# Clustered attention with a mixture of experts: scores and maxima of two key blocks in three full PSUM banks instead of four of 384 columns

## The chip, the cores and the metric

The kernel runs on one core of one Trainium2 chip. The metric is the device time of one launch in microseconds, the median of several runs. Engines are named as in the profile: PE (TensorE matmul), PEld (its weight loads), DVE (VectorE), ACT (ScalarE), POOL (GpSimd), SP (the engine that issues most DMAs). A PSUM bank holds 512 float32 columns on 128 partitions; the kernel uses six banks as a ring and two for other sums.

## The reference

Attention over 4 batches of 8 heads (sequence 768, head size 64), where a query sees only keys of its own cluster, and behind it a mixture of 8 experts of which each token uses two:

```
q_assign = argmax(q_n @ c_n.T);  k_assign = argmax(k_n @ c_n.T)      # 16 clusters per head
mask   = q_assign[..., :, None] == k_assign[..., None, :]
scores = where(mask, scale * q @ k.T, -1e9)
attn   = exp(scores - max(scores)) / (sum + 1e-9)
x      = (attn @ v) as rows of 512
top2 of x @ w_gate + noise * log1p(exp(x @ w_noise)), softmax over the two
out[token] += weight * (relu(x @ w1[e]) @ w2[e])                     # for both experts of a token
```

## The kernel before, in words

**Stages.** The 32 heads are worked on as 16 pairs (`p`), two heads (`s`) each. Attention is one long list of steps (`attention`, L378 to L393): step `t` is one block of 128 keys (`kc`, six to a head) against all 768 queries, so a pair takes 12 steps and the stage 192. The experts follow (`experts`, L949 on); nothing in them is touched.

**One step.** `scores` (L633) computes for its key block the masked scores, less the row's maximum, of all queries: two PSUM tiles of 384 columns, each from two accumulating matmuls (L641, operands `A` and `Bt`), and for each an Exp on ACT into the float32 tile `pe` (L642; 768 columns in all, six such tiles in rotation). One to three steps later `split_p` (L645) has POOL, for the last 21 blocks DVE, compute `pl`, the part of `pe` that its bfloat16 upper half leaves (L653). Four steps after the scores `values` (L656) multiplies both halves with the values: 18 matmuls of 64 or 65 columns per block into the tile `av` (L670, L672, L676); two blocks of a head fall into one step.

**Maxima.** For a later pair `b_max` (L603) computes the masked scores the other way round (128 queries against 768 keys) in two tiles of 384 columns with one matmul each (L611), and DVE takes each tile's negated row maximum (L613). `b_neg` and `b_negT` (L615, L624) bring these maxima into two rows of `Bt` by a transpose and a DMA, which the pair's first scores wait for.

**The ring.** All these tiles, and those of transposes and of small reductions, are taken in turn from six banks (`ps`, L141). A matmul into a bank waits until the tile that was six places earlier has been read, by ACT (scores) or by DVE (maxima).

**What sets the order.** Each engine executes its instructions in the order in which the program is written. The table `AT` (L27) gives to every piece of side work a step, rounded to thirds; `at` files it under step and third. The loop at L378 writes, for each step: the first third's side work, `scores`, the splits of earlier blocks, the second third, `values`, the last third. `AT["bmax"]` and `["bstep"]` place `b_max` from 9.333 steps on, one query block per step.

Of the kernel before, what the change touches and what calls it, by code (L numbers as in the profile page):

```python
# [9 lines left out]
F32 = mybir.dt.float32  # L10
# [19 lines left out]
    L=4, qk=-20.667, v=-8.667,  # L30
    vscale=-0.667, vsplit=10.667, vstep=1.0, split=[-4.667, -3.667, -4.0, -3.333], place=-0.667,
    sims=[2.0, 2.667], scales=[-14.333, -13.333, -13.0, -10.0, -8.667], scales1=2.0, max1=3.333, ge=3.667, max2=4.333, eq=4.667, mask=6.333, bmask=6.333,
    bmax=9.333, neg=20.333, negT=22.0, zero=31.0, zstep=12.0, zlist=21.0, v1=4.0, store=2.667, turn=6.667, glog=12.0,
    xh=1.333, xh0=4.0, pause=4.0, list=[34.0, 34.0, 19.0], lstep=[2.0, 2.0, 1.1667], bstep=1.0,
    gate=[13.667, 13.667, 6.333], am=5.333, amstep=0.333, xs=6.0, ky=4.0, cut=[13, 20], gplace=[30.0, 30.0, 14.333],
    vd=[1, 1, 2, 3, 4, 5], sec=-6.0, qf=[0, -4.0], place1=4.333,
# [9 lines left out]
class Kernel:  # L46
# [170 lines left out]

    def centroids(self):
        nc, D, C = self.nc, self.D, self.C
        self.early = self.wk.tile([128, 2, 384], F32, name="pe", bufs=6).rearrange("p a n -> p (a n)")  # L220
        o = 128 + 4 * C
        c1 = self.early[:, o:o + D]
        c2 = self.c2 = self.early[:, o + D:o + 3 * D].rearrange("p (a d) -> p a d", d=D)
        nc.sync.dma_start(c1, self.cent.rearrange("h c d -> (h c) d"))
        self.constants()
        n = self.early[:, o + 3 * D:o + 3 * D + 3]
        nc.vector.tensor_mul(c2[:, 0, :], c1, c1)
        nc.vector.reduce_sum(n[:, 0:1], c2[:, 0, :], axis=X)
        self.rnorm(n[:, 0:1], n[:, 1:3])
        nc.vector.tensor_scalar(c2, c1[:, None, :].to_broadcast([128, 2, D]), n[:, 0:1], None, op0=OP.mult)  # L230
# [14 lines left out]
    def attention(self, ctx):  # L245
# [20 lines left out]
        def at(step, f, *a):  # L266
            sched.setdefault(divmod(round(3 * step), 3), []).append((f, a))
# [7 lines left out]
        for p in range(NP):  # L275
            b, hp = divmod(p, H // 2)
            w = 12 * (p - 2)
            if hp == 0:
                for g in range(2):
                    at(w + T["qk"] + 24 * g + (0 if b else T["qf"][g]), self.load_qk, b, g)  # L280
                    v = w + 24 * g
                    V = T["fv"][g] if p == 0 else T
                    at(v + V["v"] + (T["v1"] if (b, g) == (1, 0) else 0), self.load_v, b, g)
                    at(v + V["vscale"], self.v_sizes, b, g)
                    chain(v + V["am"], V["amstep"], self.v_scale(b, g))
                    if g:
                        fs = self.x_scale(b)
                        chain(v + V["xs"] - (4 if b else 0), 1.0 if b else 0.333, fs[:-1])
                        at(v + V["xs"] + (2.667 if b else 3.333), fs[-1])
                    for h in range(0, 4, 2):  # L290
                        at(v + V["vsplit"] + V["vstep"] * (h + 0.667), self.v_split, b, g, h)
            P = T["first"] if p == 0 else T
            w += (0, T["sec"], T["thr"])[p] if p < 3 else 0
            if p == 0:
                for i in range(4):
                    at(w - 7.0, self.a_turn, p, i // 2, i % 2)
            if p < 2 or p % 2 == 0:
                fs = self.scales(p, 2 if p < 2 else 4)
                for x, f in zip(P["scales"], fs):
                    at(w + x + (T["scales1"] if p == 1 else 0), f)  # L300
            for i in range(4):
                at(w + P["split"][i], self.a_halves if p == 0 else self.a_split, p, i // 2, i % 2)
            if p == 0:
                at(w + P["sims"][0], self.c_turn)
            at(w + P["place"] + (T["place1"] if p == 1 else 0), self.b_place, p)
            for s in range(2):
                at(w + P["sims"][s], self.a_sims, p, s)
            for k, f in (("max1", self.a_max1), ("ge", self.a_ge), ("ky", self.a_ky), ("max2", self.a_max2),
                         ("eq", self.a_eq), ("mask", self.a_mask), ("bmask", self.b_mask)):
                at(w + P[k], f, p)  # L310
            if p == 0:
                for s in range(2):
                    for j in range(NJ):
                        at(w + P["bmax"][s] + P["bstep"][s] * j, self.b_max, p, s, j)
                    at(w + P["neg"][s], self.b_neg, p, s, 1)
                    at(w + P["negT"][s], self.b_negT, p, s, 1)
            else:
                w = 12 * (p - 2)
                bm, bs = (T["bmax1"], T["bstep1"]) if p == 1 else (T["bmax"], T["bstep"])
                for s in range(2):  # L320
                    for j in range(NJ):
                        at(w + bm + bs * (6 * s + j), self.b_max, p, s, j)
                at(w + T["neg"], self.b_neg, p, 0, 2)
                at(w + T["negT"] + (T["thr"] if p == NP - 1 else 0), self.b_negT, p, 0, 2)
            w = 12 * (p - 2)
            z = w + 36 + L
            if p + 1 < NP:
                at(z + T["xh"] + (T["xh0"] if p == 0 else 0), self.x_halves, p)
                at(z + T["store"] + (T["xh0"] if p == 0 else 0), self.store_x, p)
                turn, glog = (T["store"], 6.333) if p == NP - H // 2 - 1 else (T["turn"], T["glog"]) if p < NP - 2 else (5.0, 8.0)  # L330
                at(z + turn, self.turn_h, p)
                if p < NP - 2:
                    at(z + glog, self.g_logits, p)
            if hp == H // 2 - 1:
                if b + 1 == B:
                    continue
                fs = self.g_gate(b)
                chain(z + T["gate"][b], 0.333, fs[:8])
                for i, f in enumerate(fs[8:self.GP]):
                    x = T["gate"][b] + 2.667 + (0.333 if b < 2 else 0.1667) * i  # L340
                    at(z + x + (T["pause"] if b < 2 and x > 21 else 0), f)
                chain(z + T["gplace"][b], 0.1667, fs[self.GP:])
                for j in range(2 * NJ):
                    at(z + T["list"][b] + T["lstep"][b] * j, self.g_list, b, j)
# [7 lines left out]
        z = 12 * NP  # L352
# [25 lines left out]
        for t in range(min(sched)[0], z + L + 2):  # L378
            u = t - L
            slot = lambda i: [f(*a) for f, a in sched.pop((t, i), [])]  # L380
            slot(0)
            if 0 <= t < z:
                self.scores(t // 12, (t % 12) // 6, t % 6)
            for x in range(t - 3, t):
                if 0 <= x < z and t - x == (1 if x < z - 19 or x > z - 12 else 3 if x < z - 15 else 2):
                    self.split_p(x // 12, (x % 12) // 6, x % 6)
            slot(1)
            if 0 <= u < z:
                p, s, kc = u // 12, (u % 12) // 6, u % 6
                for i in range(NJ):  # L390
                    if AT["vd"][i] == kc:
                        self.values(p, s, i)
            slot(2)  # L393
        assert not sched

    def fixed_init(self, i):
# [203 lines left out]
                self.dma(A[64:80, i, :, 384 * a:384 * a + 384], mk[64 * i + 32 * a:64 * i + 32 * a + 16],  # L600
                         self.nc.scalar if a and p < 5 else None)

    def b_max(self, p, s, j):  # L603

        nc, st, A = self.nc, self.st[p], self.A[p % 3]
        if (s, j) == (0, 0):
            st["mm"] = self.wk.tile([128, 2 * self.NJ, 2], F32, name="mm")
        c = self.NJ * s + j
        for n in range(2):
            t = self.ps()[:, :384]  # L610
            nc.tensor.matmul(t, A[:, 0, s, j * 128:j * 128 + 128],  # L611
                             A[:, 1, s, n * 384:n * 384 + 384], start=True, stop=True)
            nc.vector.tensor_reduce(st["mm"][:, c, n:n + 1], t, axis=X, op=OP.max, negate=True)  # L613

    def b_neg(self, p, s, n):  # L615

        v, W, c = self.nc.vector, n * self.NJ, self.NJ * s
        o = self.aux[:, 500 + c:500 + c + W]
        hi, lo = (self.nm[:, W * i:W * i + W] for i in range(2))
        v.tensor_reduce(o, self.st[p]["mm"][:, c:c + W], axis=X, op=OP.min)  # L620
        v.tensor_scalar(hi, o, 1.0 / MASK, None, op0=OP.mult)
        v.scalar_tensor_tensor(lo, hi, -MASK, o, op0=OP.mult, op1=OP.add)

# [6 lines left out]
        self.dma(self.Bt[p % 3][96:98, 1, s:s + n], nt[:W], None if p else nc.scalar)  # L630


    def scores(self, p, s, kc):  # L633
        nc, st, A, Bt = self.nc, self.st[p], self.A[p % 3], self.Bt[p % 3]
        ks = slice(kc * 128, kc * 128 + 128)
        pe = self.wk.tile([128, 2, 384], F32, name="pe", bufs=6)
        for n in range(2):
            t = self.ps()[:, :384]
            ns = slice(n * 384, n * 384 + 384)
            for M, qi in ((A, 0), (Bt, 1)):  # L640
                nc.tensor.matmul(t, M[:, 1 - qi, s, ks], M[:, qi, s, ns], start=not qi, stop=bool(qi))  # L641
            nc.scalar.activation(pe[:, n], t, AF.Exp, bias=math.log(64.0), scale=st["sc"][:, 4:5])  # L642
        st["p", s, kc] = pe

    def split_p(self, p, s, kc):  # L645

        nc, st = self.nc, self.st[p]
        pe = st["p", s, kc].rearrange("p a n -> p (a n)")
        hi = pe.bitcast(BF).rearrange("p (n two) -> p n two", two=2)[:, :, 1]
        lo = self.wk.tile([128, self.S], F16, name="pl", bufs=5)  # L650

# [679 lines left out]
```

## Time and profile before

| | before |
|---|---|
| median of 3 runs (range) | 1014.69 us (1014.54 to 1014.77) |
| the profiled execution's own time | 1013.59 us |
| its span in the trace | 1011.8 us |
| granted TensorE clock, mean | 0.976 of full |
| PE, DVE, ACT, POOL busy | 92%, 65%, 47%, 56% of the span |
| attention steps | about 43 to 461 us of the span |
| experts | about 461 us to the end |

The span is what the trace covers; the execution's own time is 1.8 us more. A busy PE is not PE at its peak, since matmuls overlap in the records. The chain that ended last is followed backwards from the last instruction; its shares tell which work's duration stood on the path, not how busy an engine was.

### The profile page before, as it was taken

Reading aid. Unit: us, or ns where it says so; the run is one execution under the profiler, and the core shown is the slowest. Engines: PE = TensorE matmul, PEld = TensorE weight load, DVE = VectorE, ACT = ScalarE, POOL = GpSimd, SP = SyncE. Lnnn points to the kernel's source line nnn. Section 1 sums busy time; section 2 is a strip of 40 time slices with the busy share of each in tenths; the row PEclk is TensorE's granted clock in tenths of the full one; section 3 lists DMA queues with packets and bytes.
Section 4 is the critical chain, followed back from the end, with each engine's and each line's share of the span. In section 5 each row is a group of like instructions: output and inputs, shape, how many; then the busy total and the mean of one; then the engine's idle time right before and its main releaser. Section 6 shows DMA issues by size and latency. Waiting matters only on the chain.

```text
span 1011.8 us, 22606 instructions
## 1 busy us (share of the span) xinstructions
PE 928.7 (92%) x8825; PEld 560.4 (55%) x8825; DVE 660.6 (65%) x1485; ACT 473.4 (47%) x896; POOL 565.7 (56%) x608
## 2 busy tenths in 40 slices
PE   4588989898899987889999999999999999999997
PEld 3356666666666664668555445455454454554543
DVE  6688777888678876897556465365564654655631
ACT  4578788888787865674032224123131241231310
POOL 9268797979997899853456125242261252422312
PEclk7699999999999998999999999999999999999999
DMA  6543767666667444668377645655665356555201
GB/s 178 125 118 89 194 156 185 183 165 145 179 153 189 119 95 98 204 152 176 109 150 242 137 142 167 140 174 149 173 193 140 126 165 152 172 151 155 73 24 46
DMA packets 181905, 148.84 MB, mean 147 GB/s; under 512 B 93543, under 2 KB 159079, under 8 KB 181794
## 3 DMA queue, kind: packets, MB, share of 16 engines
q1 hardware_dynamic: 167990, 110.73, 43.8%
q0 software_dynamic: 13296, 36.38, 11.7%
q8 instruction: 70, 1.15, 0.5%
q10 hardware_dynamic: 508, 0.25, 0.1%
q14 instruction: 41, 0.34, 0.1%
HBM read 81.80 MB, written 26.12 MB: 107 GB/s over the span
## 4 chain that ended last, share of the span: by engine, by line
PE 57%; POOL 10%; DVE 9%; issue 9%; ACT 6%; DMA 4%; SPq 0%; ACTq 0%; POOLq 0%; DVEq 0%
PE ring L1230 21%; PE ring L1270 20%; POOL pl L653 6%; PE ring L641 5%; ACT pe L642 3%; DVE mm L613 3%; PE ring L611 2%; POOL tbl L899 2%; DMA B<-nt 2%; PE av L670 1%; PE av L676 1%; PE av L672 1%; POOL out L1283 1%; PE ring L1260 1%; DVE pl L653 1%
## 5 line engine op out<-in xcount | busy, mean ns | idle before, releaser
L653 POOL TENSOR_TENSOR pl<-pe 128x768 f16<-128x768 f32 x171 | 247.9, 1468 | 47.4 <-ACT pe L642 41.9
L1230 PE MATMUL ring<-xT,w1t 128*128 128x404 f16 (+2 forms) x1632 | 267.1, 324 | 0.0
L1270 PE MATMUL ring<-w2t,hT 128*128 128x512 f16 x1152 | 250.8, 379 | 0.5 <-DVE w2t L1166 0.5
L642 ACT ACTIVATE pe<-ring,sc 128x384 f32<-128x384 f32 x384 | 200.0, 577 | 69.1 <-PE ring L641 62.0
L613 DVE TENSOR_REDUCE mm<-ring 128x1 f32<-128x384 f32 x384 | 192.1, 549 | 44.6 <-PE ring L611 44.0
L1283 POOL DMA_INDIRECT out<-yo,idx x52 | 58.7, 1129 | 285.4 <-DVE yo L1279 209.3
L1230 PEld LDWEIGHTS <-w1t 128*128 128x128 f16 x1632 | 157.4, 97 | 106.4 <-issue 2.5
L1270 PEld LDWEIGHTS <-hT 128*128 128x128 f16 x1152 | 112.4, 98 | 135.0 <-issue 1.2
L1239 ACT ACTIVATE hT<-ring 128x404 f16<-128x404 f32 (+2 forms) x136 | 57.6, 469 | 202.1 <-PE ring L1230 201.9
L641 PE MATMUL ring<-B 128*128 128x384 f16 x384 | 127.2, 332 | 3.6 <-DMA B<-nt 3.6
L641 PE MATMUL ring<-A 128*128 128x384 f16 x384 | 126.8, 330 | 3.6 <-ACT pe L642 2.1
L611 PE MATMUL ring<-A 128*128 128x384 f16 x384 | 105.2, 334 | 16.5 <-ACT pe L642 8.0
L1240 DVE SCALAR_TENSOR_TENSOR hT<-ring,hT 128x404 f16<-128x404 f32 (+2 forms) x136 | 66.7, 529 | 73.5 <-ACT hT L1239 73.5
L1279 DVE SCALAR_TENSOR_TENSOR yo<-ring,lsw,xt 128x512 f32<-128x512 f32 (+1 forms) x49 | 36.7, 748 | 110.2 <-PE ring L1270 104.3
L670 PE MATMUL av<-vv,pe 128*128 128x65 f16 x1152 | 96.9, 194 | 7.5 <-DVE xt L685 7.4
L672 PE MATMUL av<-vv,pe 128*128 128x64 f16 x1152 | 96.9, 193 | 0.0
L670 PEld LDWEIGHTS <-pe 128*128 128x128 bf16 x1152 | 83.7, 98 | 22.9 <-issue 9.3
L1165 ACT ACTIVATE w1t<-stg,ws 128x1024 f16<-128x1024 f32 x32 | 34.5, 1139 | 121.2 <-DVE ws L170 121.2
L672 PEld LDWEIGHTS <-pe 128*128 128x128 bf16 x1152 | 78.4, 99 | 11.3 <-issue 4.7
L676 PE MATMUL av<-vv,pl 128*128 128x65 f16 x1152 | 66.8, 194 | 5.6 <-POOL pl L653 4.2
L1210 POOL DMA_INDIRECT xh<-xs,idx x52 | 56.4, 1085 | 16.5 <-issue 15.0
L1154 DVE TENSOR_REDUCE wm<-stg 128x1 f32<-128x1024 f32 x56 | 65.5, 1208 | 0.0
(227 smaller groups left out, 1171.0 us busy)
## 6 DMA issues: line engine op xcount, KB each, us to landing
stg<-in_moe_w SPq DMA_DIRECT2D x64, 512.0 KB
vt<-in_v SPq DMA_DIRECT2D x8, 768.0 KB
out<-zt SPq DMA_DIRECT2D x12, 512.0 KB
A<-hl SPq DMA_DIRECT2D x30, 192.0 KB
B<-hl SPq DMA_DIRECT2D x30, 192.0 KB
xs<-xh SPq DMA_DIRECT2D x15, 384.0 KB
qk<-in_q SPq DMA_DIRECT2D x7, 768.0 KB
qk<-in_k SPq DMA_DIRECT2D x7, 768.0 KB
```

The source lines that it names most:

```text
L611: nc.tensor.matmul(t, A[:, 0, s, j * 128:j * 128 + 128], A[:, 1, s, n * 384:n * 384 + 384], start=True, stop=True)
L613: nc.vector.tensor_reduce(st["mm"][:, c, n:n + 1], t, axis=X, op=OP.max, negate=True)
L641: nc.tensor.matmul(t, M[:, 1 - qi, s, ks], M[:, qi, s, ns], start=not qi, stop=bool(qi))
L642: nc.scalar.activation(pe[:, n], t, AF.Exp, bias=math.log(64.0), scale=st["sc"][:, 4:5])
L653: (nc.vector if last else nc.gpsimd).tensor_tensor(lo, pe, hi, op=OP.subtract)
L670: nc.tensor.matmul(av[:, j, :], ph[:, js], vv[:, hh, kj, 64:129], start=(kc == 0 and j == 0), stop=False, skip_group_check=True)
L672: nc.tensor.matmul(av[:, j, :64], ph[:, js], vv[:, hh, kj, 0:64], start=False, stop=False, skip_group_check=True)
L676: nc.tensor.matmul(av[:, j, :], pl[:, js], vv[:, hh, kj, 64:129], start=False, stop=(kc == NJ - 1), skip_group_check=True)
L1230: nc.tensor.matmul(p, self.w1t[:, wi, c, f * 128:f * 128 + 128], self.xT[:, c, xi, n0:n1], start=(i == 0), stop=(i == 3 * ND - 1))
L1240: nc.vector.scalar_tensor_tensor(h1, x, 0.0, h0, op0=OP.max, op1=OP.subtract)
L1270: nc.tensor.matmul(p, self.hT[:, hi, f, t * 128:t * 128 + 128], self.w2t[:, wi, f], start=(i == 0), stop=(i == 3 * NF - 1))
L1283: i = nc.gpsimd.indirect_dma_start(out=self.out, out_offset=bass.IndirectOffsetOnAxis(ap=en[:r], axis=0), in_=yo[:r], in_offset=None, boun ...
```

## The change

Two key blocks of a head now share one `pe` tile of 1536 columns (four in rotation instead of six of 768) and three PSUM tiles of 512 columns: the first holds 512 queries' columns of the even block, the second the even block's last 256 and the odd block's first 256, the third the odd block's last 512. `pieces` yields the parts of a tile. Each tile gets one Exp of 512 columns. The three tiles are written at three places: the first at the start of the even step, the second at its end, the third in the odd step behind the splits. `b_max` does the same for two query blocks: three tiles of 512 columns, one reduction each (the middle tile's gives two columns of maxima), placed every 2/3 of a step instead of two tiles every step; `AT["bmax"]` becomes 9.0. `b_neg` reads the same 24 maxima, laid out flat. `early` is the tile of `pe`'s name that the constants use at the start.

```diff
-    bmax=9.333, neg=20.333, negT=22.0, zero=31.0, ...
+    bmax=9.0, neg=20.333, negT=22.0, zero=31.0, ...
...
-                    for j in range(NJ):
-                        at(w + bm + bs * (6 * s + j), self.b_max, p, s, j)
+                    for j in range(3 * NJ // 2):
+                        at(w + bm + bs * (9 * s + j) * 2 / 3, self.b_max, p, s, j)
...
-            if 0 <= t < z:
-                self.scores(t // 12, (t % 12) // 6, t % 6)
+            score = lambda i: 0 <= t < z and self.scores(t // 12, (t % 12) // 6, t % 6 // 2, i)
+            if t % 2 == 0:
+                score(0)
             for x in range(t - 3, t):
                 if 0 <= x < z and t - x == (1 if x < z - 19 or x > z - 12 else 3 if x < z - 15 else 2):
                     self.split_p(x // 12, (x % 12) // 6, x % 6)
+            if t % 2:
+                score(2)
             slot(1)
...
             slot(2)
+            if t % 2 == 0:
+                score(1)
...
+    def pieces(self, c, i):
+        S = self.S
+        x = 512 * i
+        while x < 512 * i + 512:
+            y = min(512 * i + 512, (x // S + 1) * S)
+            yield c + x // S, x % S, x - 512 * i, y - x
+            x = y
...
-        for n in range(2):
-            t = self.ps()[:, :384]
-            nc.tensor.matmul(t, A[:, 0, s, j * 128:j * 128 + 128],
-                             A[:, 1, s, n * 384:n * 384 + 384], start=True, stop=True)
-            nc.vector.tensor_reduce(st["mm"][:, c, n:n + 1], t, axis=X, op=OP.max, negate=True)
+        jj, i = divmod(q, 3)
+        t = self.ps()
+        for j, x, o, n in self.pieces(2 * jj, i):
+            nc.tensor.matmul(t[:, o:o + n], A[:, 0, s, j * 128:j * 128 + 128], A[:, 1, s, x:x + n], start=True, stop=True,
+                             skip_group_check=True)
+        c = 2 * self.NJ * s + 4 * jj + (0, 1, 3)[i]
+        k = 2 if i == 1 else 1
+        nc.vector.tensor_reduce(st["mm"][:, c:c + k], t.rearrange("p (k n) -> p k n", k=k), axis=X, op=OP.max, negate=True)
...
-        pe = self.wk.tile([128, 2, 384], F32, name="pe", bufs=6)
-        for n in range(2):
-            t = self.ps()[:, :384]
-            ns = slice(n * 384, n * 384 + 384)
-            for M, qi in ((A, 0), (Bt, 1)):
-                nc.tensor.matmul(t, M[:, 1 - qi, s, ks], M[:, qi, s, ns], start=not qi, stop=bool(qi))
-            nc.scalar.activation(pe[:, n], t, AF.Exp, bias=math.log(64.0), scale=st["sc"][:, 4:5])
-        st["p", s, kc] = pe
+        if i == 0:
+            pe = self.wk.tile([128, 2 * S], F32, name="pe", bufs=4)
+            for k in range(2):
+                st["p", s, 2 * kk + k] = pe[:, S * k:S * k + S]
+            st["pe"] = pe
+        t = self.ps()
+        for kc, x, o, n in self.pieces(2 * kk, i):
+            ks = slice(kc * 128, kc * 128 + 128)
+            for M, qi in ((A, 0), (Bt, 1)):
+                nc.tensor.matmul(t[:, o:o + n], M[:, 1 - qi, s, ks], M[:, qi, s, x:x + n], start=not qi, stop=bool(qi),
+                                 skip_group_check=True)
+        nc.scalar.activation(st["pe"][:, 512 * i:512 * i + 512], t, AF.Exp, bias=math.log(64.0), scale=st["sc"][:, 4:5])
```

How it moves PE's instructions. Before, in an attention step of a late pair (the scores of one key block, L641, then the maxima of one query block, L611; `A` and `Bt`, here B, are the operands, each matmul behind its weight load):

```order
L641 LDWEIGHTS A_132
L641 MATMUL ring<-A_132 128x384
L641 LDWEIGHTS B_135
L641 MATMUL ring<-B_135 128x384
L641 LDWEIGHTS A_132
L641 MATMUL ring<-A_132 128x384
L641 LDWEIGHTS B_135
L641 MATMUL ring<-B_135 128x384
L611 LDWEIGHTS A_133
L611 MATMUL ring<-A_133 128x384
L611 LDWEIGHTS A_133
L611 MATMUL ring<-A_133 128x384
```

With the change, at the turn from an even to an odd step: the middle tile of the scores (L660, two parts of 256), a tile of maxima (L625) and the third tile of the scores, whose second matmul, of B, follows:

```order
L660 LDWEIGHTS A_132
L660 MATMUL ring<-A_132 128x256
L660 LDWEIGHTS B_135
L660 MATMUL ring<-B_135 128x256
L660 LDWEIGHTS A_132
L660 MATMUL ring<-A_132 128x256
L660 LDWEIGHTS B_135
L660 MATMUL ring<-B_135 128x256
L625 LDWEIGHTS A_133
L625 MATMUL ring<-A_133 128x512
L660 LDWEIGHTS A_132
L660 MATMUL ring<-A_132 128x512
```

Two tiles of scores now stand close together around a tile of maxima, with no matmuls of `values` between them; the even block is complete only with the middle tile. The number of matmuls is the same.

On ACT, over some steps in which it also builds the next pair's mask (L577), its operand halves (L524) and a row of maxima (L629). Before:

```order
L642 ACTIVATE pe<-ring,sc 128x384 x2
L577 ACTIVATE mk<-ring,ms 128x768
L642 ACTIVATE pe<-ring,sc 128x384 x2
L524 ACTIVATE hl<-ring,sc 128x384 x2
L642 ACTIVATE pe<-ring,sc 128x384 x2
L524 ACTIVATE hl<-ring,sc 128x384 x2
L642 ACTIVATE pe<-ring,sc 128x384 x2
L629 ACTIVATE nt<-ring 24x128
```

With the change (the same places are L662, L582, L529 and L645):

```order
L662 ACTIVATE pe<-ring,sc 128x512
L582 ACTIVATE mk<-ring,ms 128x768
L662 ACTIVATE pe<-ring,sc 128x512 x2
L529 ACTIVATE hl<-ring,sc 128x384 x2
L662 ACTIVATE pe<-ring,sc 128x512
L529 ACTIVATE hl<-ring,sc 128x384 x2
L662 ACTIVATE pe<-ring,sc 128x512 x2
L645 ACTIVATE nt<-ring 24x128
```

Where ACT had two Exps in every step, it has one in even and two in odd steps.

## Rows read from the trace of the kernel before

**Rows 1.** Windows: engine busy us (instructions), granted clock, DMA share, GB/s, by stretch.

```profile
core 0: us, PE busy (x) PEld busy (x) DVE busy (x) ACT busy (x) POOL busy (x), PEclk, DMA share, GB/s
43.00:461.00 418.00, 368.74 (x5686) 263.87 (x5686) 343.14 (x891) 318.36 (x593) 344.40 (x297) 0.98 0.62 152
...
235.00:280.00 45.00, 37.66 (x560) 27.16 (x557) 34.54 (x91) 34.94 (x65) 43.01 (x46) 1.00 0.67 163
...
337.00:385.00 48.00, 42.24 (x673) 30.98 (x670) 36.03 (x92) 33.30 (x62) 46.04 (x48) 0.98 0.53 118
...
461.00:1011.00 550.00, 541.17 (x2997) 283.36 (x2994) 291.26 (x525) 135.23 (x266) 193.66 (x282) 1.00 0.52 143
```

**Rows 2.** Chain that ended last: whole span, then 100 to 235, then 235 to 280.

```profile
by line: PE ring L1230 21.4%; PE ring L1270 20.0%; issue 8.5%; POOL pl L653 5.7%; PE ring L641 4.5%; ACT pe L642 3.2%; DVE mm L613 2.5%; PE ring L611 2.3%; POOL tbl L899 1.6%; DMA B<-nt 1.5%; PE av L670 1.5%; PE av L676 1.4%; PE av L672 1.4
...
by line: PE ring L641 16.7%; ACT pe L642 9.8%; PE ring L611 8.4%; DMA B<-nt 8.2%; issue 5.3%; PE av L670 4.7%; PE av L676 4.6%; PE av L672 4.5%; DVE mm L613 3.4%; PE ring L511 3.4%; DMA qk<-in_q 3.2%; ACT junk L178 3.1%; ACT hl L524 2.5%; D
...
by line: POOL pl L653 58.1%; POOL tbl L899 18.4%; POOL xh L721 7.1%; issue 6.0%; ACT pe L642 3.6%; PE ring L641 1.9%; DVE xt L685 1.3%; PE av L670 0.7%; POOL ch L455 0.6%; DVE rs L682 0.5%; POOL spacer L898 0.5%; DVE rs L683 0.5%; PE ring L
```

**Rows 3.** Costliest groups: shapes, count | busy us, mean ns | idle before, releasers.

```profile
L653 POOL TENSOR_TENSOR pl<-pe 128x768 f16<-128x768 f32 x171 | 247.9, 1468 | 47.4 <-ACT pe L642 41.9 <-ACT nt L629 2.2 <-ACT gm L829 2.1
L642 ACT ACTIVATE pe<-ring,sc 128x384 f32<-128x384 f32 x384 | 200.0, 577 | 69.1 <-PE ring L641 62.0 <-POOL pl L653 3.8 <-PE ring L611 1.7
L613 DVE TENSOR_REDUCE mm<-ring 128x1 f32<-128x384 f32 x384 | 192.1, 549 | 44.6 <-PE ring L611 44.0
```

**Rows 4.** Waits, 43 to 461: engine line <- releaser: us, times, longest us.

```profile
ACT pe L642 <- PE ring L641: 62.0, 77, 2.2
...
PEld L641 <- issue: 21.5, 64, 1.4
PEld L611 <- issue: 9.8, 24, 1.4
...
PE ring L611 <- ACT pe L642: 8.0, 24, 1.1
...
PEld L676 <- POOL pl L653: 5.1, 7, 1.0
...
PE av L676 <- POOL pl L653: 4.2, 6, 0.9
...
PE ring L641 <- ACT pe L642: 2.1, 3, 1.2
...
PE ring L611 <- DVE mm L613: 1.5, 2, 1.1
```

**Rows 5.** Groups by form: other lengths from PSUM on ACT and DVE.

```profile
L1239 ACT ACTIVATE hT<-ring 128x404 f16<-128x404 f32 x56 | 28.5, 508 | 169.5 <-PE ring L1230 169.5
...
L1239 ACT ACTIVATE hT<-ring 128x256 f16<-128x256 f32 x24 | 8.8, 381 | 32.5 <-PE ring L1230 32.4
...
L160 DVE TENSOR_REDUCE pr<-ring 128x1 f32<-128x128 f32 x15 | 4.2, 281 | 0.0
```

**Rows 6.** Timeline: start us, us, engine line op, count [idle before]; a full ring.

```profile
127.40 1.98 ACT L642 ACTIVATE pe<-ring,sc 128x384 f32<-128x384 f32 x4
...
128.02 0.32 PE L611 MATMUL ring<-A 128*128 128x384 f16 x1 [1.06 <-ACT pe L642]
...
138.84 3.07 DVE L613 TENSOR_REDUCE mm<-ring 128x1 f32<-128x384 f32 x6
```

**Rows 7.** Pieces of the chain: start us, us, what; matmuls of 384, 256 and 512 columns.

```profile
164.25 0.65 PE ring L641 x4
...
460.63 7.87 PE ring L1230 x72
...
492.27 15.55 PE ring L1270 x72
```

More of the change, by code (lines that the diff above doesn't have):

```diff
@@ L32 @@
     sims=[2.0, 2.667], scales=[-14.333, -13.333, -13.0, -10.0, -8.667], scales1=2.0, max1=3.333, ge=3.667, max2=4.333, eq=4.667, mask=6.333, bmask=6.333,
-    bmax=9.333, neg=20.333, negT=22.0, zero=31.0, zstep=12.0, zlist=21.0, v1=4.0, store=2.667, turn=6.667, glog=12.0,
+    bmax=9.0, neg=20.333, negT=22.0, zero=31.0, zstep=12.0, zlist=21.0, v1=4.0, store=2.667, turn=6.667, glog=12.0,
     xh=1.333, xh0=4.0, pause=4.0, list=[34.0, 34.0, 19.0], lstep=[2.0, 2.0, 1.1667], bstep=1.0,
@@ L219, in centroids @@
         nc, D, C = self.nc, self.D, self.C
-        self.early = self.wk.tile([128, 2, 384], F32, name="pe", bufs=6).rearrange("p a n -> p (a n)")
+        self.early = self.wk.tile([128, 2 * self.S], F32, name="pe", bufs=4)
         o = 128 + 4 * C
@@ L312, in attention @@
                 for s in range(2):
-                    for j in range(NJ):
-                        at(w + P["bmax"][s] + P["bstep"][s] * j, self.b_max, p, s, j)
+                    for j in range(3 * NJ // 2):
+                        at(w + P["bmax"][s] + P["bstep"][s] * j * 2 / 3, self.b_max, p, s, j)
                     at(w + P["neg"][s], self.b_neg, p, s, 1)
@@ L320, in attention @@
                 for s in range(2):
-                    for j in range(NJ):
-                        at(w + bm + bs * (6 * s + j), self.b_max, p, s, j)
+                    for j in range(3 * NJ // 2):
+                        at(w + bm + bs * (9 * s + j) * 2 / 3, self.b_max, p, s, j)
                 at(w + T["neg"], self.b_neg, p, 0, 2)
@@ L601, in b_mask, with b_max @@
                          self.nc.scalar if a and p < 5 else None)
-    def b_max(self, p, s, j):
-        nc, st, A = self.nc, self.st[p], self.A[p % 3]
-        if (s, j) == (0, 0):
-            st["mm"] = self.wk.tile([128, 2 * self.NJ, 2], F32, name="mm")
-        c = self.NJ * s + j
-        for n in range(2):
-            t = self.ps()[:, :384]
-            nc.tensor.matmul(t, A[:, 0, s, j * 128:j * 128 + 128],
-                             A[:, 1, s, n * 384:n * 384 + 384], start=True, stop=True)
-            nc.vector.tensor_reduce(st["mm"][:, c, n:n + 1], t, axis=X, op=OP.max, negate=True)
+    def pieces(self, c, i):
[5 more added lines that the diff above has]
+            x = y
+    def b_max(self, p, s, q):
+        nc, st, A = self.nc, self.st[p], self.A[p % 3]
+        if (s, q) == (0, 0):
+            st["mm"] = self.wk.tile([128, 4 * self.NJ], F32, name="mm")
+        jj, i = divmod(q, 3)
[6 more added lines that the diff above has]
+        nc.vector.tensor_reduce(st["mm"][:, c:c + k], t.rearrange("p (k n) -> p k n", k=k), axis=X, op=OP.max, negate=True)
     def b_neg(self, p, s, n):
@@ L619, in b_neg @@
         hi, lo = (self.nm[:, W * i:W * i + W] for i in range(2))
-        v.tensor_reduce(o, self.st[p]["mm"][:, c:c + W], axis=X, op=OP.min)
+        v.tensor_reduce(o, self.st[p]["mm"][:, 2 * c:2 * c + 2 * W].rearrange("p (j n) -> p j n", n=2), axis=X, op=OP.min)
         v.tensor_scalar(hi, o, 1.0 / MASK, None, op0=OP.mult)
@@ L630, in b_negT, with scores @@
         self.dma(self.Bt[p % 3][96:98, 1, s:s + n], nt[:W], None if p else nc.scalar)
-    def scores(self, p, s, kc):
-        nc, st, A, Bt = self.nc, self.st[p], self.A[p % 3], self.Bt[p % 3]
-        ks = slice(kc * 128, kc * 128 + 128)
-        pe = self.wk.tile([128, 2, 384], F32, name="pe", bufs=6)
-        for n in range(2):
-            t = self.ps()[:, :384]
-            ns = slice(n * 384, n * 384 + 384)
+    def scores(self, p, s, kk, i):
+        nc, st, A, Bt, S = self.nc, self.st[p], self.A[p % 3], self.Bt[p % 3], self.S
+        if i == 0:
[6 more added lines that the diff above has]
+            ks = slice(kc * 128, kc * 128 + 128)
             for M, qi in ((A, 0), (Bt, 1)):
-                nc.tensor.matmul(t, M[:, 1 - qi, s, ks], M[:, qi, s, ns], start=not qi, stop=bool(qi))
-            nc.scalar.activation(pe[:, n], t, AF.Exp, bias=math.log(64.0), scale=st["sc"][:, 4:5])
-        st["p", s, kc] = pe
+                nc.tensor.matmul(t[:, o:o + n], M[:, 1 - qi, s, ks], M[:, qi, s, x:x + n], start=not qi, stop=bool(qi),
+                                 skip_group_check=True)
+        nc.scalar.activation(st["pe"][:, 512 * i:512 * i + 512], t, AF.Exp, bias=math.log(64.0), scale=st["sc"][:, 4:5])
     def split_p(self, p, s, kc):
         nc, st = self.nc, self.st[p]
-        pe = st["p", s, kc].rearrange("p a n -> p (a n)")
+        pe = st["p", s, kc]
         hi = pe.bitcast(BF).rearrange("p (n two) -> p n two", two=2)[:, :, 1]
```

## The prediction

> **What bounds the kernel now.** I read the windows first. From 461 us on PE is busy in 541 of 550 us [rows 1]: the experts are PE's, the change touches nothing there, and what attention gains or loses passes on whole. In the attention steps, 43 to 461 us, nobody is full: of 418 us PE is busy 369, POOL 344, DVE 343, ACT 318 [rows 1]. So no engine's total sets this stage; four engines in fixed orders hand tiles to each other, and which hand-over ends last changes from stretch to stretch.
>
> Next the chain of waits. Over the span it lies 4.5% on the matmuls of the scores, 3.2% on the Exp, 2.5% on the reductions of the maxima, 2.3% on their matmuls [rows 2]. Between 100 and 235 us it runs to and fro between PE and ACT; between 235 and 280 it is POOL's, 58.1% on the splits alone [rows 2], with POOL busy for 43.0 of 45 us, and 337 to 385 looks the same with 46.0 of 48 [rows 1]. These 93 us the change can hardly touch: POOL's splits stay as they are, 171 of 1468 ns [rows 3].
>
> Last the waits. ACT's Exp waited for PE 77 times, 62.0 us in all, yet PE also waited for ACT to empty a bank: 24 times, 8.0 us, before a matmul of the maxima, 2.1 us before one of the scores, and 1.5 us for DVE [rows 4], 11.6 us together. One such place is plain: at 127.40 ACT comes out of other work with four Exps in a row, and PE, its six banks full, stands still for 1.06 us until one is free [rows 6]. Each side waits for the other at times; that is what a short ring between two engines with uneven side work looks like.
>
> **The change part by part.**
>
> *Exp.* 384 of 384 columns become 288 of 512. No Exp of 512 stands in this trace. Between 256 and 404 columns an ACT read of PSUM goes from 381 to 508 ns, 0.86 ns a column [rows 5]; 128 more columns make 577 [rows 3] into 687 ns. Two key blocks cost 4 x 577 = 2308 ns before and 3 x 687 = 2061 after, 10.7% less. Back to back the four take 1.98 us [rows 6], (1.98 - 0.577) / 3 = 468 ns for each further one; 4 x 468 against 3 x 578 is 7.4% less. The chain has 3.2% of 1011.8 = 32.4 us of Exp, so the path shortens by 2.4 to 3.5 us; I take **3.5**, since most Exps there follow a wait. Outer ends: nothing (ACT off the path), or 96 pairs of blocks x 0.247 = 23.7 us if ACT alone bound the stage, which its 318 of 418 us excludes.
>
> *Reductions.* From 128 to 384 columns a reduction goes from 281 [rows 5] to 549 ns [rows 3], 1.05 ns a column, so 512 take 683: 3 x 683 against 4 x 549 is 6.7% less. In a row of six each further one takes (3.07 - 0.55) / 5 = 504 ns [rows 6]; 3 x 638 against 4 x 504 is 5% less. Of 2.5% = 25.3 us on the chain that is 1.3 to 1.7 us; I take **1.5**. The shorter end of a pair's last maxima, one reduction where two stood, is in it.
>
> *The ring.* In two steps scores and maxima took eight tiles and now take six: the whole ring turns once in two steps, and PE may run a third more columns ahead of the slower reader. PE's visible waits for a bank are 11.6 us. Between nothing and all of it I take a quarter, **3**, because the same moments are partly counted as Exp on the chain. The weight loads held back by "issue", 21.5 and 9.8 us [rows 4], have no releaser in the records; I give them no price.
>
> *A longer hand-over.* Against this, ACT must now wait for a full bank: two matmuls of 512 columns instead of 384. Four of 384 take 0.65 us, 72 of 512 take 15.55 [rows 7]: 2 x 216 = 432 ns against 325, 107 more. If every wait of ACT for PE (77, of which three quarters are left) stood on the path, this would cost 58 x 0.107 = 6.2 us. But ACT's waits are mostly PE's own busy time (`values`, side matmuls), when nobody loses; I take **1**.
>
> *PE's work.* Same number of matmuls and weight loads, same columns. Parts of 256 run at 7.87 / 72 = 109 ns, 0.43 ns a column, as 384 and 512 do (0.42) [rows 7]: nothing, and no cover is needed.
>
> *Tiles and order.* A `pe` tile comes back after eight steps instead of six, which can only help the 3.8 us that the Exp waited for POOL's split [rows 3]; nothing counted. The even block is complete with the middle tile, at the end of its step instead of its start, so its split can start about a step later. It is used four steps after the scores, and POOL takes 1468 ns a block where a step lasts 418 / 192 = 2.18 us. Where POOL is behind it does not wait, and where it is not, some two steps are left. Nothing counted; what hides it is that reserve. If it ran out, `values` would wait for `pl`, which now costs 5.1 + 4.2 = 9.3 us [rows 4].
>
> Sum: -3.5 - 1.5 - 3 + 1 = **-7.0 us** of the profiled execution's 1013.59, so 1006.6. That execution is 1.1 us under the median of the runs; against the median the forecast is 1014.69 - 7.0 = **1007.7 us**.
>
> **A rule that speaks against it.** ACT is busy 76% and DVE 82% of the stage [rows 1], and both still hold PE up at times [rows 4]. The Trainium skill (Perfetto Trace Analysis, Optimizing Scalar/DVE Operations) says that larger operations improve throughput where the engine is saturated, and that where it is not but causes bubbles elsewhere, breaking instructions up may let work finish sooner. This trace has both: ACT is not saturated over the stage, but is for stretches like that at 127 us. By the rule's second half alone the change would lose; that is the second rival below, priced from rows.
>
> **The rivals.**
>
> 1. *The gain is absorbed.* ACT and DVE are sped up, and POOL or PE's own work ends last in their place. For: POOL's 43.0 of 45 us and PE's 88% over the stage. Against: where the chain runs between PE and ACT, ACT's share is real work. Only the reductions' 1.5 us would be left: 1014.69 - 1.5 = 1013.2 us. Chance 0.18.
>
> 2. *The hand-over decides (slower).* Place: PE to ACT and back, where the chain runs between them as from 100 to 235 us [rows 2]. Each wait of ACT for a bank grows by 107 ns, each wait of PE for ACT or DVE by the 110 ns of a longer Exp. If the waits stay on the path and the ring gains nothing: -3.5 - 1.5 + 6.2 + (24 + 3 + 2) x 0.11 = +4.4, so 1019.1 us. It decides from the point where over four in five of ACT's waits leave PE without other matmuls (-5 + 6.2 over nothing). Against: `values` and the side matmuls stand between. Chance 0.11.
>
> 3. *The late even block.* POOL comes too late with every even block's split and the waits of `values` for `pl` double: -7 + 9.3 = +2.3, 1017.0 us. Against: two steps of reserve. Chance 0.07.
>
> 4. *The ring gives all.* All 11.6 us of PE's waits for banks go, and the 3.8 of Exp for POOL: -3.5 - 1.5 - 11.6 - 3.8 + 1 = -19.4, 995.3 us. For: six tiles in two steps is the ring exactly. Against: POOL's 93 us don't shrink, and other tiles (transposes, mask, logits) still shift the turn. Chance 0.12.
>
> That the change does not do what it says I exclude: the order shows the new lengths.
>
> **How the numbers follow.** The forecast has the remaining 0.52. What a measurement of this kernel can tell from no change is about 0.2%, 2 us: faster is under 1012.7, slower over 1016.7. Faster: nearly all of the forecast (0.50), all of rival 4 (0.12), a third of rival 1 (0.06), 0.68. Same: the rest of rival 1 and of the forecast, and a part of rival 3, 0.16. Slower: rival 2 and the greater part of rival 3, 0.16. The range from 998 to 1017 us takes in the unknown sizes of the Exp and ring terms and rival 1, and leaves out most of rivals 2 and 4, less than 2 in 10.
>
> **What would show it.** Right, if Exps of 512 columns take about 690 ns and reductions about 680; if PE's waits for banks under the maxima and scores fall well below 11.6 us; if the experts' part keeps its length; and if the stretches in which POOL leads keep theirs. Wrong, if ACT's idle time before the Exp grows beyond 62 us by more than what ACT saves, if `pl` shows as releaser of PE for much more than 9.3 us, or if POOL's share of the chain takes over what ACT gives up.

## The result, and the profile after

| | before | after |
|---|---|---|
| median of 5 runs (range) | 1014.54 us (1013.2 to 1014.77) | 1003.96 us (1002.95 to 1008.5) |
| ratio after to before, 95% interval | | 0.9906 (0.9882 to 0.993) |

The change makes the kernel 10.6 us faster; 7.0 were forecast, and 1003.96 lies within the range of 998 to 1017. The execution profiled with this result is the slowest of the five, 1008.5 us. The changed kernel was profiled again in the first experiment below, in an execution of 1004.03 us, near the median; the lines of after are from that one.

The windows, with the stage cut where attention ends (columns as in [rows 1]):

```profile
43.00:452.00 409.00, 359.50 (x5691) 265.04 (x5691) 336.67 (x800) 306.36 (x497) 341.56 (x297) 0.98 0.63 156
452.00:1002.00 550.00, 540.60 (x2992) 282.84 (x2989) 290.69 (x523) 135.27 (x266) 193.04 (x282) 1.00 0.51 142
```

The experts take 550 us as before [rows 1], and all of the gain lies in attention. ACT has 12 us less to do than in [rows 1], DVE 6.5.

The costliest groups of the three instructions the change speaks of:

```profile
L672 POOL TENSOR_TENSOR pl<-pe 128x768 f16<-128x768 f32 x171 | 247.1, 1467 | 50.6 <-ACT pe L662 38.1
...
L662 ACT ACTIVATE pe<-ring,sc 128x512 f32<-128x512 f32 x288 | 189.5, 685 | 71.1 <-PE ring L660 57.5
...
L629 DVE TENSOR_REDUCE mm<-ring 128x1 f32<-128x512 f32 (+1 forms) x288 | 190.7, 683 | 36.8 <-PE ring L625 36.4
```

An Exp of 512 columns takes 685 ns and a reduction 683, where 687 and 683 were worked out. Against [rows 3], ACT is busy 10.5 us less with Exps; DVE's reductions, which overlap in the records, 1.4 us less.

The chain that ended last, over the whole span:

```profile
by line: PE ring L1249 21.7%; PE ring L1289 20.2%; issue 8.9%; POOL pl L672 4.8%; PE ring L660 3.5%; DVE mm L629 3.4%; PE ring L625 1.7%; DMA B<-nt 1.7%; POOL tbl L918 1.6%; ACT pe L662 1.4%; PE av L695 1.2%; PE av L689 1.2%; PE av L691 1.1
```

In [rows 2] the Exp had 3.2%, the scores 4.5%, the reductions 2.5%. The Exp has lost more than half of its share of the path, and the reductions have gained some: DVE came up next.

The waits between 43 and 452 us:

```profile
ACT pe L662 <- PE ring L660: 57.5, 73, 2.1
...
PEld L625 <- issue: 13.2, 20, 2.2
PEld L660 <- issue: 12.8, 36, 1.1
...
PEld L695 <- POOL pl L672: 9.3, 12, 1.3
...
PE av L695 <- POOL pl L672: 7.7, 10, 1.2
...
PE ring L660 <- ACT pe L662: 1.8, 4, 0.9
...
PE ring L625 <- ACT pe L662: 1.7, 5, 0.7
```

PE's waits for a bank of scores or maxima to be read fall from 8.0 + 2.1 + 1.5 = 11.6 us [rows 4] to 1.8 + 1.7 = 3.5. The weight loads held back by "issue" fall from 31.3 to 26.0 us. The place of [rows 6], ACT coming out of the scaling of values, looks like this now:

```profile
123.94 0.84 ACT L473 ACTIVATE vv<-vt 128x768 f16<-128x768 f32 x1
124.69 1.82 ACT L662 ACTIVATE pe<-ring,sc 128x512 f32<-128x512 f32 x3
```

ACT still catches up with Exps in a row, three now for two blocks, and no idle time of PE of 0.1 us or more stands in the trace between 120 and 132 us, where [rows 6] had 1.06.

Where along the way the time was won is read from the ends of heads, the timeline's writes into `xt`. Before:

```profile
236.99 0.56 DVE L685 TENSOR_TENSOR xt<-av,rs 128x384 f32<-128x384 f32 x1
...
278.97 0.56 DVE L685 TENSOR_TENSOR xt<-av,rs 128x384 f32<-128x384 f32 x1
...
343.79 0.56 DVE L685 TENSOR_TENSOR xt<-av,rs 128x384 f32<-128x384 f32 x1
...
385.57 0.56 DVE L685 TENSOR_TENSOR xt<-av,rs 128x384 f32<-128x384 f32 x1
...
461.29 0.56 DVE L685 TENSOR_TENSOR xt<-av,rs 128x384 f32<-128x384 f32 x1
```

And after, the same heads:

```profile
228.55 0.56 DVE L704 TENSOR_TENSOR xt<-av,rs 128x384 f32<-128x384 f32 x1
...
271.87 0.56 DVE L704 TENSOR_TENSOR xt<-av,rs 128x384 f32<-128x384 f32 x1
...
332.78 0.56 DVE L704 TENSOR_TENSOR xt<-av,rs 128x384 f32<-128x384 f32 x1
...
375.91 0.56 DVE L704 TENSOR_TENSOR xt<-av,rs 128x384 f32<-128x384 f32 x1
...
451.72 0.56 DVE L704 TENSOR_TENSOR xt<-av,rs 128x384 f32<-128x384 f32 x1
```

The lead is 8.4 us at the first of these heads, 7.1 at the second, 11.0, 9.7 and 9.6 at the others. It grows while PE, ACT and DVE hand tiles to each other, and shrinks by 1.3 us in each of the two stretches that POOL leads (42.0 us became 43.3, and 41.8 became 43.1). From 385 us of the kernel before on it stays as it is.

### The profile page after: what moved, and what is told of

Same layout as the page of the kernel before. It is cut to its first block, busy times and chain, and to the rows that moved or that the text cites. A ratio compares the mean times of both kernels' runs of the same rounds, so it can differ in the third digit from the quotient of the medians.

```text
span 1006.7 us, 22293 instructions
## 1 busy us (share of the span) xinstructions
PE 921.0 (91%) x8825; PEld 562.6 (56%) x8825; DVE 653.8 (65%) x1389; ACT 461.6 (46%) x800; POOL 559.3 (56%) x608
## 4 chain that ended last, share of the span: by engine, by line
PE 56%; DVE 13%; issue 9%; POOL 8%; ACT 4%; DMA 3%; POOLq 0%; DVEq 0%; ACTq 0%; SPq 0%
PE ring L1249 22%; PE ring L1289 20%; PE ring L660 4%; POOL pl L672 4%; DVE mm L629 4%; DMA B<-nt 2%; PE ring L625 2%; ACT pe L662 2%; PE av L695 1%; PE av L689 1%; POOL tbl L918 1%; PE av L691 1%; POOL out L1302 1%; PE ring L1279 1%; DVE xt L704 1%
## 5 line engine op out<-in xcount | busy, mean ns | idle before, releaser
L662 ACT ACTIVATE pe<-ring,sc 128x512 f32<-128x512 f32 x288 | 189.7, 685 | 75.7 <-PE ring L660 62.7
L629 DVE TENSOR_REDUCE mm<-ring 128x1 f32<-128x512 f32 (+1 forms) x288 | 190.7, 683 | 40.3 <-PE ring L625 39.9
L660 PE MATMUL ring<-B 128*128 128x512 f16 (+1 forms) x384 | 122.9, 333 | 4.0 <-DMA B<-nt 4.0
L660 PE MATMUL ring<-A 128*128 128x512 f16 (+1 forms) x384 | 122.6, 333 | 3.3 <-ACT pe L662 1.8
L625 PE MATMUL ring<-A 128*128 128x512 f16 (+1 forms) x384 | 111.3, 337 | 11.0 <-ACT pe L662 2.6
L1229 POOL DMA_INDIRECT xh<-xs,idx x52 | 53.9, 1037 | 16.6 <-issue 15.3
```

The costliest lines, as they stand in the source:

```text
L625: nc.tensor.matmul(t[:, o:o + n], A[:, 0, s, j * 128:j * 128 + 128], A[:, 1, s, x:x + n], start=True, stop=True, skip_group_check=True)
L629: nc.vector.tensor_reduce(st["mm"][:, c:c + k], t.rearrange("p (k n) -> p k n", k=k), axis=X, op=OP.max, negate=True)
L660: nc.tensor.matmul(t[:, o:o + n], M[:, 1 - qi, s, ks], M[:, qi, s, x:x + n], start=not qi, stop=bool(qi), skip_group_check=True)
L662: nc.scalar.activation(st["pe"][:, 512 * i:512 * i + 512], t, AF.Exp, bias=math.log(64.0), scale=st["sc"][:, 4:5])
```

## The experiments

The theory after the result: the gain has three parts, ACT's shorter Exps, DVE's fewer reductions, and the ring, which holds a third more columns. Rivals: one of the parts is nearly all of it; the finer mixing of the order makes it; or the longer rotation of `pe` does. All were timed against the kernel before on their own chip. Except for the last run, before stood at 1014.7 to 1015.0 us there.

**1. The change again.** The file is unchanged.

> The changed kernel once more, for its scatter and a second profile. If the first profile (1008.5 us, the slowest of five) shows an ordinary execution, the heads end as there: 9 us ahead of the kernel before at 335 us, 5 ahead at the end of attention. If the 3 to 4 us that it lost between 360 and 420 us are an accident of that execution, this one is some 4 us shorter and keeps 8 to 10 us to the end. Median 1003 to 1005 us either way.

Measured: 1003.79 us (1003.22 to 1004.38) against 1015.04, ratio 0.988 (0.9857 to 0.9903). It keeps a lead of 9.6 us to the end of attention; what the first profiled execution lost was its own. Against this run the others are read.

**2. Scores alone.** `b_max`, `b_neg`, the loops that place the maxima and `bmax` as before:

```diff
-    bmax=9.0,
+    bmax=9.333,
...
-        for j, x, o, n in self.pieces(2 * jj, i):
+        for n in range(2):
+            t = self.ps()[:, :384]
```

> The scores and Exps as changed, the maxima as before (384 columns, bmax at 9.333). By the forecast's terms the Exp (3.5 us) and about half of the ring (1.5) are left, less the longer hand-over (1): 4 us faster than before, 1010.5. If the ring is the larger part of the gain, two tiles of maxima per step keep half of the turn and the gain is about half of the measured 10.6: 1009. If the shorter Exp is nearly all, 1005.

Measured: 1010.37 us, ratio 0.9938 (0.9914 to 0.9962): 4.7 us faster than before.

**3. Maxima alone.** The kernel before with the change's `b_max`, `b_neg`, placing and `bmax`.

> The maxima as changed, the scores and Exps as before. By the forecast's terms the reductions (1.5 us) and half of the ring (1.5) are left: 3 us faster than before, 1011.5. If the reductions count for more than the chain showed (DVE led much of the late stage), 6 to 8 us faster; if the maxima were hidden, no change, 1014.

Measured: 1009.83 us, ratio 0.9942 (0.9921 to 0.9963): 5.2 us faster. Neither half is hidden and neither is all of it; 4.7 and 5.2 add up to 9.9 of the 11.2 us by which run 1 beat the same runs of before. The maxima are worth more than the 3 us of the forecast's terms.

**4. Four Exps again, all else as changed.**

```diff
-        nc.scalar.activation(st["pe"][:, 512 * i:512 * i + 512], t, AF.Exp, ...)
+        w = 256 if i == 1 else 512
+        for o in range(0, 512, w):
+            nc.scalar.activation(st["pe"][:, 512 * i + o:512 * i + o + w], t[:, o:o + w], AF.Exp, ...)
```

> The change, but the middle tile's Exp made as two of 256 columns: 4 Exps per two blocks again, tiles, ring and order as changed. By the slope of the forecast two blocks then cost ACT 2 x 687 + 2 x 467 = 2308 ns, as before the change. If ACT's time is worth the forecast's term, 3.5 us slower than the change, 1007.5; if ring and order make the gain, at most 1 us slower, 1004 to 1005; if ACT's time is nearly all of it, 8 to 10 us slower.

The groups by form show the price that was set, 2 x 688 + 2 x 472 = 2320 ns for two blocks, 2308 before the change:

```profile
L664 ACT ACTIVATE pe<-ring,sc 128x512 f32<-128x512 f32 x192 | 131.9, 688 | 43.0 <-PE ring L660 39.0 <-POOL spacer L919 1.4 <-POOL pl L674 1.1
...
L664 ACT ACTIVATE pe<-ring,sc 128x256 f32<-128x256 f32 x192 | 80.4, 472 | 20.6 <-PE ring L660 16.4 <-PE ring L516 3.2
```

Measured: 1004.99 us, ratio 0.9895 (0.9871 to 0.9919), 1.2 us slower than run 1. The intervals overlap, so in the changed kernel ACT's shorter Exps are a small part of the gain at most. The split gave nothing back by an earlier start: in none of the 96 middle tiles does the first half's Exp begin before the tile's last matmul has ended.

**5 and 6. Places of the ring passed over.** The middle tiles of the scores and of the maxima each took one more tile and left it unused (the same edit at both places); run 6 also split the middle Exp and reduction, as run 7 does.

```diff
+        if i == 1:
+            self.ps()
         t = self.ps()
```

> The change, but the middle tile of the scores and of the maxima each passes over one place of the ring unused: eight places in two steps again, so that the six banks hold no more columns ahead than before. Instructions and their order as changed. If the longer ring is the larger part of the gain, 5 to 7 us slower than the change, 1009 to 1011; by the forecast's term 3 us slower, 1007; if the gain comes from the new order of the work or from shorter ACT and DVE time, no change, 1004.

> The ring's places passed over as in the run before it, and the middle tiles' Exp and reduction made as two of 256 columns: ring, Exp and reductions as dear as before, only the tile layout and the order are the change's. If these three terms are the whole gain, 1013 to 1015, as before the change. If the order or the shorter waits between engines count by themselves, what remains of the 11 us shows it: 1008 to 1011.

Measured: 1002.9 us (ratio 0.9891, 0.9871 to 0.9911) and 1008.58 us (0.994, 0.9924 to 0.9956). These two tell nothing on the ring: the tile that nobody writes took no place in it. On every engine the instructions of run 5, and the semaphores that they wait for, are those of the change, so it is the change once more, as run 6 repeats run 7. PE's waits for a bank read by the Exp are 1.8 and 1.7 us in run 5 too.

**7. Four Exps and four reductions again.** As run 4, and in `b_max`:

```diff
-        nc.vector.tensor_reduce(st["mm"][:, c:c + k], t.rearrange("p (k n) -> p k n", k=k), axis=X, op=OP.max, negate=True)
+        for x in range(k):
+            w = 512 // k
+            nc.vector.tensor_reduce(st["mm"][:, c + x:c + x + 1], t[:, w * x:w * x + w], axis=X, op=OP.max, negate=True)
```

> The change with the middle tiles' Exp and reduction both made as two of 256 columns, ring as changed. The split Exp alone cost 1 to 1.5 us. If reductions are worth the forecast's 1.5 us, 1006.5 to 1007; if DVE's time is worth more, as the shares of the late chain suggest, 1008 to 1010; if neither counts, 1005.

Measured: 1008.49 us, ratio 0.9939 (0.9925 to 0.9953). The reductions are worth some 3.5 us (1008.49 - 1004.99), more than twice the forecast. Runs 1 and 4 stood on another chip than run 7; beside run 5, the change on run 7's own chip, Exps and reductions together are worth 5.6 us instead of 4.7. With Exps and reductions as many as before, 6.5 us of gain are left, and PE's waits for banks stay as short as with the change:

```profile
PE ring L662 <- ACT pe L666: 1.9, 4, 0.9
...
PE ring L625 <- ACT pe L666: 1.9, 5, 0.7
```

**8. The kernel before with five banks.** The number stands at two places, of which one is shown.

```diff
-        return self.psum.tile([128, 512], F32, name="ring", bufs=6)
+        return self.psum.tile([128, 512], F32, name="ring", bufs=5)
```

> The kernel before with five banks in the ring instead of six. If the ring is what held it, a sixth less of it costs 6 us or more, 1021 and over; by the forecast's 3 us for a third more ring, about 1.5 to 3 us, 1017; if the ring does not matter, 1015.

Measured: 1030.26 us, ratio 1.0149 (1.0132 to 1.0165): 15 us slower, all of it in attention, whose last head ends 16.5 us later. PE's waits for banks of scores and maxima are 30.3 us, 11.6 with six banks:

```profile
PE ring L611 <- ACT pe L642: 20.6, 58, 1.9
...
PE ring L641 <- ACT pe L642: 5.0, 7, 1.2
...
PE ring L611 <- DVE mm L613: 2.5, 1, 2.5
PE ring L641 <- DVE mm L613: 2.2, 3, 1.0
```

**9. The change with five banks.** The same edit in the changed kernel.

> The change with five banks in the ring instead of six: 2560 columns ahead, where the kernel before had 2304 with six banks and 1920 with five. If the ring's length in columns is the gain that is left when Exps and reductions are as dear as before (6.5 us), a good part of it goes, 3 to 6 us slower than the change, 1007 to 1010, and far less than the 15 us that one bank was worth before. If the ring is long enough by now, no change, 1004. If the number of banks counts and not their columns, 15 us slower, 1019.

Measured: 1011.35 us, ratio 0.996 (0.9946 to 0.9974): 7.6 us slower than run 1, more than the 3 to 6 us expected. The waits for banks come back to 4.6 + 3.9 + 1.9 + 0.4 = 10.8 us, about what they were before the change:

```profile
PE ring L660 <- ACT pe L662: 4.6, 15, 0.6
...
PE ring L625 <- ACT pe L662: 3.9, 15, 0.7
...
PE ring L660 <- DVE mm L629: 1.9, 1, 1.9
```

The chain moves back as well, with Exps and reductions as the change has them: the Exp from 1.4% to 2.5% (3.2% before the change), the reductions from 3.4% to 2.2% (2.5% before):

```profile
by line: PE ring L1249 21.5%; PE ring L1289 20.0%; issue 8.6%; PE ring L660 4.7%; POOL pl L672 4.6%; ACT pe L662 2.5%; DVE mm L629 2.2%; PE ring L625 1.9%; POOL tbl L918 1.6%; PE av L689 1.5%; PE av L695 1.5%; PE av L691 1.4%; DMA B<-nt 1.2
```

This run, read with run 7, is the strongest on the cause. It is 3.4 us faster than the kernel before (2.6 to 5.5 by its interval), and that is no more than the 4.7 us of Exps and reductions. If the prices add up, little or nothing (at most 5.5 - 4.7 = 0.8 us) is left of the 6.5 us once PE waits for banks as before, although the new order, the layout of the tiles and the rotation of `pe` are all still there.

By the columns that the banks hold, the times are 1920 columns 1030.3 us, 2304 1015.0, then, with the change's Exps and reductions, 2560 1011.4 and 3072 1003.8. Columns alone do not order them: without the 4.7 us, the 2560 columns in five banks would stand near 1016 us (an estimate), no better than 2304 in six. How many banks there are counts too.

**10. Three `pe` tiles instead of four**, six blocks in rotation as before.

```diff
-        self.early = self.wk.tile([128, 2 * self.S], F32, name="pe", bufs=4)
+        self.early = self.wk.tile([128, 2 * self.S], F32, name="pe", bufs=3)
...
-            pe = self.wk.tile([128, 2 * S], F32, name="pe", bufs=4)
+            pe = self.wk.tile([128, 2 * S], F32, name="pe", bufs=3)
```

> The change with three tiles of pe in rotation instead of four, six blocks as before the change. If the longer life of pe is part of the gain, 2 to 5 us slower, 1006 to 1009 (the Exp waited 3.8 us for POOL's split before the change); if not, 1004.

Measured: 1003.64 us, ratio 0.989 (0.9875 to 0.9905), as the change. The rotation of `pe` gives nothing; the fourth tile is spare.

**11. The order alone, spoilt.** In the kernel before, `b_max` takes one tile at a time, at half steps from 8.667 on, and the second tile of the scores stands later in the step:

```diff
+            if 0 <= t < z:
+                self.scores(t // 12, (t % 12) // 6, t % 6, 0)
...
             slot(1)
+            if 0 <= t < z:
+                self.scores(t // 12, (t % 12) // 6, t % 6, 1)
```

> The kernel before, tiles of 384 and ring as they were, but in the change's manner of order: the second tile of the scores behind the splits, the maxima one tile at a time at half steps instead of two together. If the finer mixing of the order is what is left of the gain, 4 to 6.5 us faster than before, 1009 to 1011; if it is the ring's columns, no change, 1015.

Measured: 1160.44 us, ratio 1.1429 (1.1413 to 1.1445). This answers another question. In the last step of a pair the second third holds the DMA that lays a later pair's operand into `A`. The moved tile stands behind it: it is computed from the later pair's data, and PE waits for the DMA to land. The waits between 43 and 605 us:

```profile
PE ring L644 <- DMA A<-hl: 116.4, 13, 11.7
```

13 pairs, 9 us each. The run says nothing on the finer order.

**12. The order alone, mended.** The second tile stands ahead of that third in a pair's last step, behind it in all others.

```diff
+            if 0 <= t < z and t % 12 == 11:
+                self.scores(t // 12, (t % 12) // 6, t % 6, 1)
             slot(1)
+            if 0 <= t < z and t % 12 < 11:
+                self.scores(t // 12, (t % 12) // 6, t % 6, 1)
```

> The order experiment again without the stall of the run before, where a pair's last tile of scores stood behind the DMA that overwrites its operand: in the last step of a pair the second tile now stands ahead of that DMA, in all others behind the side work of the second third. Tiles of 384, ring, Exps and reductions as in the kernel before; only their order is mixed as finely as the change's. If order is what is left of the gain, 4 to 6.5 us faster than before, 1008 to 1011; if the ring's columns are, within 2 us of before, 1013 to 1017; worse if tiles that come later in the step cost the ring more.

Measured, on a chip where all runs were longer and scattered more: 1045.33 us (1037.59 to 1055.29) against 1040.94 for the kernel before, ratio 1.0013 (0.9972 to 1.0053). The interval leaves out a gain of more than 3 us. PE's waits for banks grew (10.9 + 4.7 + 3.9 + 1.8 = 21.3 us), so the ring was not held as it was, and a gain by the order could be hidden behind them. Shown is that this finer mixing, on a ring of 384 columns a tile, does not give the 6.5 us that are left; it is also not quite the order of the change.

## Why the prediction was right, and where its terms were off

**The direction and the place.** Right. The gain lies in attention and reaches the end whole: 9.6 us at its last head, 10.6 to 11.3 in the time. The forecast of 7.0 is a third too small. That it came as near is in part luck: the Exp, 2.3 us too high, makes up for the reductions, 2.0 too low, and what the sum lacks is the ring's.

**The durations.** Right to 2 ns: a slope from two neighbouring forms of the same engine and memory was enough.

**Exp, forecast 3.5 us.** Mis-sized. Splitting the middle Exp gave ACT its old load back and cost 1.2 us (run 4). The forecast multiplied the Exp's 32.4 us on the chain by its shortening. But nearly half of those pieces, 14.9 us, lead straight to a matmul of PE into the ring, that is to a bank that became free; with the change 0.7 us of such pieces are left, and the Exp has 1.4% of the chain instead of 3.2%. The same Exps of 512 columns have 2.5% with five banks (run 9). So most of what the Exp lost on the path, some 14 of 18 us, it lost by the ring and not by its length.

**Reductions, forecast 1.5 us.** Mis-sized the other way: 3.5 us (run 7 against run 4). Their share rose from 2.5 to 3.4% of the chain: with the banks' waits gone DVE ends last more often, and with five banks it is back at 2.2% (run 9). A share of the chain before does not hold for the chain after. Both prices are of the changed kernel; what fewer Exps alone would be worth in the kernel before, with its ring, was not tried.

**The ring, forecast 3 us.** Too small, and the largest part. 6.5 us remain with Exps and reductions as before (run 7). PE's waits for banks fell from 11.6 to 3.5 us; with one bank taken away they are back at 10.8, and by the prices of run 7 little or nothing of the 6.5 us is left (run 9). The rotation of `pe` gives nothing (run 10), and a finer order alone did not give it either (run 12, within the limits named there). That the remainder is the ring is thus shown by its coming and going with the waits for banks, not by a run that changes the columns alone; and it rests on prices of separate runs adding up. The forecast's term was a quarter of the 11.6 us, held down for fear of counting the Exp twice. It was the other way round: in good part the Exp was counted where the ring belonged.

**The longer hand-over, forecast -1 us.** Contained in the 6.5 us and not measured by itself. ACT's waits for PE went from 62.0 us in 77 to 57.5 us in 73. So rival 2 fell. The half of the Trainium skill's rule that spoke for it (Perfetto Trace Analysis, Optimizing Scalar/DVE Operations) says that breaking up the instructions of an engine that is not saturated but holds up others may let work finish sooner; the runs here do not bear that out. The change goes the other way and gains, and run 7, which breaks up the middle tiles' instructions at the same ring, is 4.7 us slower than run 1, although ACT is busy only 306 of 409 us. Most of that is the reductions'; and since none of run 7's halves of an Exp begins before its tile's last matmul has ended, an earlier start, which could speak for the rule, was not tried.

**PE's work at nothing.** Nothing contradicts it: PE is busy 369 us of the stage in [rows 1] and 360 after, with as many matmuls.

**Rival 1, the gain absorbed.** In part: POOL's two stretches, which the forecast wanted to keep their length, each gave 1.3 us back. The stretch after the first of the heads above holds 44 of POOL's instructions now and held 43 before; POOL is no faster, and PE comes to it earlier.

**Rival 3, the late even block.** PE's waits for `pl` did go from 9.3 [rows 4] to 17.0 us, about double, as this rival had it; the prediction named that as a sign of being wrong. It came another way. They all lie in POOL's two stretches: 228 to 272 and 333 to 376 us hold all 22 of them. There POOL is busy for 42.0 of 44 and 41.2 of 43 us, and none of its waits there is for a tile of `pe`, so no late block held it up:

```profile
228.00:272.00 44.00, 35.72 (x535) 26.23 (x534) 31.82 (x75) 33.29 (x54) 42.00 (x44) 1.00 0.65 166
333.00:376.00 43.00, 35.61 (x547) 26.42 (x546) 31.02 (x71) 27.05 (x44) 41.19 (x44) 0.96 0.51 113
```

The others simply arrive earlier at a POOL that is not faster, and wait there. That the reserve of two steps held in the other stretches fits this: no wait of PE for POOL's `pl` lies there.

**Rival 4, the ring gives all.** Its mechanism was nearer than its chance of 0.12 said, since 8.1 of the 11.6 us of waits went and 6.5 us of time with them; its sum of 995.3 us was further off than the forecast's.

## What to carry to other kernels

Where several engines are each 75 to 90% busy and hand tiles to each other through a short ring, see first whether the tiles fill the ring's buffers: full banks make the same ring hold more, and here that was worth more than the instructions that it saved. Before a change, price the ring by taking one buffer away: 15 us for one bank of six showed at once how much hangs on it, which the chain's shares hid. It is not the price of a longer ring; a third more columns gave some 6.5 us. A step's place in the order carries its DMAs too, as the 13 waits of 9 us in run 11 show; and a buffer that is only named, as in runs 5 and 6, is not taken.

## What was not expected of the hardware

The same kind of extra work had a very different price on two engines, at the same ring. The 96 Exps more of run 4 cost the kernel 1.2 us, though they give ACT 96 x (2320 - 3 x 685) ns = 25 us more of Exp durations, while the 96 reductions more of run 7 cost some 3.5 us at 96 x (2 x 682 + 2 x 414 - 3 x 683) ns = 14 us more of durations: a quarter of it landed for DVE, a twentieth for ACT. The first of the two differences is within the overlap of the intervals of runs 1 and 4. Why ACT hid more of it is not shown.
